# A two-layer long-convolution and MLP kernel: k read as plain rows, four tokens to a partition, ten products on GpSimd, a new written order

## The chip, the core and the metric

The kernel runs on one core of a Trainium2 chip. Its engines are TensorE (PE in the profile, with its weight loads as PEld), VectorE (DVE), ScalarE (ACT), GpSimd (POOL) and SyncE (SP), which here only issues DMAs. The metric is device time in microseconds (us); lower is better.

## The reference

Two blocks are applied twice to x, which starts as q (2048 tokens of 512 channels, bf16).

```python
k_shift = sum over t in 0..3 of k_pad[:, t:t+S] * shift_k[:, 3-t]     # k_pad: 3 zeros, then k
kv = k_shift * v
y  = irfft(rfft(kv, 2S) * rfft(ssm_k, 2S))[:S] + kv * ssm_D          # long causal convolution
A(x) = layernorm(x) * y
B(x) = gelu(layernorm(x) @ w1 + b1) @ w2 + b2                        # 512 -> 1376 -> 512
x = x + A(layernorm(x)); x = x + B(layernorm(x));  the same two lines again
```

y doesn't depend on x: both layers use the same y.

## The kernel before

The 2048 tokens are cut into four blocks j of 512 tokens. Filter block j and kv block j are each brought to 512 frequencies. Output block j is the sum over a of the product of kv block a and filter block j - a, brought back to time. The names below are the pieces of the list `ORDER`, in which the order on every engine is written out by hand: a piece is `name.engine`, and engines S, A, D, G, P are SP, ACT, DVE, POOL and PE. Each engine takes its instructions strictly in that order. PE writes to four PSUM buffers P0 to P3.

- `lK`, `lk`, `lv`, `lx` load blocks of the filter, k, v and q. `lT` loads the tables of the direct transform, `lF`, `lW`, `lM`, `lY` the others. `lk` is a transposing DMA from DRAM (line 330): channels come to lie on partitions.
- `KT` turns the filter block on PE (line 383), `KTe` copies it out. `dt` adds ssm_D to the filter's first token, so the kv * ssm_D term costs nothing further.
- `kv` (line 405) forms the shifted sum on PE: k against diagonal matrices `DG` of the four taps, 56 matmuls a half block, in 64x64 tiles. `kvm` (line 416) multiplies by v; the result is u.
- For blocks 0 and 1, `KD` and `UD` (line 442) transform the filter and u directly, with eight 128x512 matmuls a piece.
- For blocks 2 and 3 the transform has two steps. `KS`, `US` (line 467) do the first; `Kw`, `Uw` write its result to DRAM, `Kr`, `Ur` read it back in another order, and `KW`, `UW` (line 483) do the second step. This write and read is called a round trip below.
- `ks` (line 427) swaps real and imaginary halves of a filter block by DMA from SBUF to SBUF.
- `T` (line 503) are the products of one u block with one filter block, all on DVE. `V` (line 516) sums them and does the first inverse step; `Vw`, `Vr` are its round trip; `Y` (line 535) the second step.
- In layer l, block g has number i = 2g + l. `sa`/`sb` (line 260 and on) are the layer norm statistics on DVE, `pa`/`pb` (line 272) the inverse root on POOL, `aa`/`ab` (lines 280, 282) the normalising on ACT or DVE, `ga` (lines 593, 594) x + norm * y. `dw` writes the normalised block to DRAM and `dr` (line 605) reads it back transposed; block 0 of layer 0 is turned on PE instead (`LT`, line 576).
- `m1` (line 617) and `ge` (line 624) are the first MLP matrix and gelu, `m2` (line 637) the second. `re` (line 645) adds the residual on DVE; for i = 0 and 1 PE adds it with an identity matmul (line 634) and `re` is a plain copy (line 241 on ACT). `st` stores.

Partition p of k, u, the filter and x holds tokens 8(p mod 64) + 4(p div 64) + 0..3 of its block: a load or store needs two DMAs of 64 partitions.

Of the kernel before, what the change touches and what calls it, by code (L numbers as in the profile page):

```python
# [16 lines left out]
ls.A id.G lK0.S lk0.S lD.A lT2.A ke0.G id2.D lb.G lT0.A lY.A lT3.A w3.S lx0.S lT1.A dg.D lv0.S sg.G lx2.S KT00.P0 lK1.S  # L17
KT01.P1 KT00e.D KT01e.A dt.D lF.A kv01.P2 ke1.G KD02.P3 KD03.P0 KD02e.D sa00.D kv00.P1 KD03e.A lM.A ks011.S KD00.P3
sa02.D ks010.S lx1.S KD01.P0 KD00e.A kvm00.D kvm01.D KT10.P3 KD01e.A sa40.D UD02.P1 ks000.S lk1.S sa42.D pa40.G UD03.P2
UD02e.A pa00.G KT10e.A lK3.S ks001.S T002.D UD01.P0 pa42.G lv1.S sa22.D UD03e.A w2.S KD11.P1 UD01e.A ke2.G pa02.G T003.D  # L20
aa40.A KD10.P3 pa22.G T001.D UD00.P2 aa42.A aa22.D KD10e.D kv11.P0 UD00e.A KD11e.D V01.P3 V02.P2 kvm11.D ks101.S kv10.P1
V02e.A ks100.S T000.D V01e.A V03.P0 lK2.S KD13.P2 lv2.S kvm10.D V03e.A aa02.A Vw01.S V00.P3 T100.D KD12.P0 V00e.A
UD10.P1 KD12e.D aa00.A Vw00.S KD13e.D UD11.P3 UD10e.A sa20.D ks110.S UD13.P0 UD11e.A ks111.S lW.A T110.D UD12.P2 UD13e.A
Vr00.S Vr01.S lk2.S KT20.P1 T101.D UD12e.A KT20e.A w1.S w4.S Y00.P3 T111.D V10.P0 Y00e.A Y01.P2 V11.P1 Y01e.A ga00.D
KS23.P3 V11e.A V13.P2 ga02.D V10e.A V12.P1 KS23e.A sb00.D kv20.P0 Vw10.S V13e.A KS21.P3 sb02.D V12e.A KT30.P2 KS21e.A
Vw11.S kv21.P1 kvm20.D pb02.G KT30e.A KS20.P3 pb00.G ab02.D cb.G pa20.G ab00.D LT02.P0 KS20e.A KS22.P2 kvm21.D on0.G
LT02e.A Vr10.S LT00.P3 Vr11.S LT00e.D US21.P1 KS22e.A US20.P0 US20e.D m102.P3 US21e.A Kw21.S T213.D US22.P2 ge02.A
US23.P0 m103.P1 aa20.D US23e.A US22e.D Y11.P3 ge03.A m101.P0 T210.D Uw21.S Kw20.S Uw20.S Y11e.A T211.D Y10.P2 ge01.A
m105.P1 Y10e.D m100.P3 ge05.A ga20.D m104.P0 ge00.A Kr2.S T212.D KS31.P2 ge04.A KS30.P1 sb20.D KS32.P3 m200.P0 KS32e.A
Ur2.S KS31e.A sb22.D pb20.G KS30e.A ab20.D pb22.G dw20.S ke3.G ab22.D KW20.P3 dw22.S re00.A KW22.P2 KW20e.D Kw30.S  # L30
KW23.P1 KW23e.A KS33.P0 KW22e.D UW23.P3 UW23e.A KW21.P1 sa10.D UW21.P2 KS33e.A m202.P3 dr2.S UW21e.A KW21e.D pa10.G
aa10.A T221.D ks200.S ks201.S T223.D lv3.S Kw31.S m125.P0 re02.A UW20.P2 UW22.P1 sa12.D m120.P3 UW22e.A UW20e.A m124.P1
T201.D pa12.G ge25.A aa12.A T200.D V21.P2 T222.D m123.P0 V21e.A Kr3.S ga10.D lk3.S m122.P2 ge23.A T220.D ge24.A m121.P0
T203.D ge22.A V20.P1 T202.D ge20.A V23.P2 sb10.D V20e.A V22.P3 ge21.A Vw20.S lx3.S sb12.D pb10.G kv30.P1 V22e.A on2.G
V23e.A pb12.G KW33.P0 kvm30.D kv31.P3 KW33e.A Vw21.S KW32.P2 kvm31.D KW30.P1 ab12.A m220.P0 ab10.D KW30e.A sa62.D dw12.S
dw10.S KW32e.A Vr20.S T323.D pa62.G US33.P3 re20.D US32.P1 m222.P2 US32e.A dr1.S T313.D US33e.A T320.D Uw31.S Vr21.S
T311.D US30.P0 re22.D US31.P1 US30e.A m112.P3 aa62.D US31e.A T322.D KW31.P2 ge12.A Y20.P0 Uw30.S m110.P1 sa32.D KW31e.A
m115.P3 Y20e.A ks301.S T312.D Y21.P2 ge10.A m111.P0 Ur3.S sa30.D Y21e.A ks300.S m113.P1 ge15.A T310.D pa30.G ge11.A
on1.G m114.P2 ga40.D pa32.G ge13.A ge14.A UW30.P3 sb42.D on4.G UW33.P0 UW31.P1 UW30e.A m212.P2 UW33e.A T301.D pb42.G
UW31e.A sb40.D ab42.A T321.D pb40.G dw42.S m210.P3 re12.A T300.D ab40.A T330.D T303.D aa30.A dw40.S T331.D UW32.P0  # L40
T302.D V31.P1 UW32e.A dr4.S aa32.D V30.P2 T332.D V31e.A re10.A T333.D V32.P0 V30e.A sa60.D Vw30.S V33.P1 V32e.D pa60.G
m141.P3 V33e.A ga30.D Vw31.S m142.P2 ge41.A aa60.D m140.P0 sb30.D ge42.A m143.P1 Vr31.S ge40.A sb32.D pb30.G Vr30.S
m144.P3 ge43.A pb32.G ab32.D m145.P2 ge44.A ab30.D dw32.S Y31.P0 ge45.A dw30.S Y30.P1 st10.S Y31e.A Y30e.D m242.P3
st12.S ga60.D dr3.S sb62.D m240.P2 sb60.D pb60.G pb62.G ab60.D m131.P0 ab62.D re40.D dw62.S dw60.S m130.P1 sa50.D
m134.P2 ge30.A re42.D pa50.G ge31.A dr6.S m133.P1 sa52.D ge34.A m135.P3 aa50.D ge33.A pa52.G m132.P0 aa52.A m165.P2
m163.P1 ge32.A ga50.D ge65.A m162.P0 ge35.A ge63.A sb50.D m164.P2 sb52.D m160.P3 pb52.G m161.P1 ge60.A on3.G ab52.D
# [13 lines left out]
T202:622 T212:1286 T222:558 vs21:1415 T203:1463 T213:966 T223:1030 ziV2:1254 y2:878 x2:750 T300:1254 T310:1574 T320:1478  # L60
T330:1190 vs30:312 T301:518 T311:1414 T321:1286 T331:1222 T302:910 T312:1510 T322:1446 T332:582 vs31:518 T303:280
T313:1382 T323:1350 T333:550 ziV3:0 y3:88 x3:1030 W1:344 W2:128 ln0:1190 lt0:1222 h0:558 ln2:646 lt2:646 h2:878 ln4:1062
lt4:248 h4:430 ln6:1318 lt6:32 h6:430 ln1:1383 lt1:1542 h1:910 ln3:216 lt3:0 h3:216 ln5:304 lt5:518 h5:0 ln7:304 lt7:88
h7:430
# [17 lines left out]
def _make_tables():  # L82
# [11 lines left out]
    for h in range(2):  # L94
        rows = slice(64 * h, 64 * h + 64)
        F[rows, 0, 0], F[rows, 0, 1] = c, s
        F[rows, 1, 0], F[rows, 1, 1] = s, -c

# [77 lines left out]
def kernel(ctx: ExitStack, tc: tile.TileContext, A_q, A_k, A_v, A_shift_k, A_ssm_k, A_ssm_D,  # L176
# [75 lines left out]
    class Norm:  # L252
# [10 lines left out]


# [6 lines left out]
        def root(self, a, b):  # L271
            nc.gpsimd.tensor_tensor(self.rs[:, a:b], self.rs[:, a:b], mhalf[:, a:b], ALU.pow)  # L272

        def apply(self, eng, dst, xg, a, b):
            if eng == "A":
                nc.vector.scalar_tensor_tensor(out=self.nm[:, a:b], in0=self.mv[:, a:b, 0], scalar=-1.0, in1=self.rs[:, a:b],  # L276
                                               op0=ALU.mult, op1=ALU.mult)
# [26 lines left out]
    with tc.tile_pool(name="ps", bufs=1, space=bass.MemoryType.PSUM) as ps:  # L304
# [21 lines left out]
        PAD = 16  # L326
        KW = PAD + L

        def k_turn(it, j):
            nc.sync.dma_start_transpose(at(f"kT{j}", PAD, [[KW, CT], [1, L]]), k_d[L * j:L * j + L, :])  # L330
        q_d, k_d, v_d, out_d = (t.flatten_outer_dims() for t in (A_q, A_k, A_v, out))
        lk, edge = [], []
        for j in range(NB):
            lk.append(add(f"lk{j}", "S", [], lambda it, j=j: k_turn(it, j), kb=[512], xbar=True, bufs=[buf(f"kT{j}", CT * KW)]))

            def left(it, j=j):
                dst = at(f"kT{j}", PAD - 4, [[KW, CT], [1, 4]])
                if j == 0:
                    nc.gpsimd.memset(dst, 0.0)
# [344 lines left out]
```

## Time and profile before

| | us |
|---|---|
| median of 3 runs | 276.62 (274.1 to 276.82) |
| the profiled execution, its own time | 278.13 |
| its span, first to last instruction | 276.4 |
| outside the span | 1.7 |
| PE busy in the span | 245.8 |
| DVE busy | 174.8 |
| ACT busy | 143.0 |
| POOL busy | 34.9 |
| mean granted PE clock | 0.983 |

The profile shows one execution. Busy PE time isn't PE at full rate: matmuls overlap, so counts of instructions in a stretch say more than busy time does. A line number is that of the kernel before; several pieces can share a line where a helper records them (line 241 is every copy on ACT, line 313 every plain load).

### The profile page before, as it was taken

How to read it: one execution, taken by the hardware profiler on the slowest of the kernel's cores; microseconds unless marked ns; L12 is line 12 of the kernel's file. 1: busy time of each engine (PE TensorE's matmuls, PEld its weight loads, DVE VectorE, ACT ScalarE, POOL GpSimd, SP SyncE). 2: the span in 40 equal slices, each digit the busy share in tenths (PEclk: the TensorE clock that was granted, in tenths of full speed). 3: DMA queues.
4: the chain of work that ended last, by engine and by line, in shares of the span. 5: the costliest groups of instructions: out<-in, count | busy, mean ns of one | idle time of the engine just before them, and what ended most of it. 6: DMA issues, size and time to landing. Idle time of an engine off the chain costs nothing.

```text
span 276.4 us, 4777 instructions
## 1 busy us (share of the span) xinstructions
PE 245.8 (89%) x1921; PEld 119.7 (43%) x1944; DVE 174.8 (63%) x306; ACT 143.0 (52%) x184; POOL 34.9 (13%) x59
## 2 busy tenths in 40 slices
PE   1179998979999959999999799999999999999991
PEld 1045546444834424446433245444444444444440
DVE  0209659779887875895979598948955148611041
ACT  1102458576888666695578575570394502802700
POOL 4000330000400200010205120112104011200000
PEclk9999999997999999999999799999999999999998
DMA  7999797999677979797989323593410230051034
GB/s 124 147 238 233 187 239 205 275 302 222 220 225 239 235 218 225 175 221 217 191 266 219 84 75 80 170 287 76 123 34 1 76 78 0 31 121 38 2 86 104
DMA packets 46794, 43.46 MB, mean 157 GB/s; under 512 B 25554, under 2 KB 41524, under 8 KB 46004
## 3 DMA queue, kind: packets, MB, share of 16 engines
q1 hardware_dynamic: 45010, 41.63, 59.3%
q10 hardware_dynamic: 1682, 1.53, 3.4%
q8 instruction: 15, 0.25, 0.4%
q0 software_dynamic: 80, 0.00, 0.1%
q14 instruction: 7, 0.06, 0.1%
HBM read 19.03 MB, written 14.16 MB: 120 GB/s over the span
## 4 chain that ended last, share of the span: by engine, by line
PE 59%; DMA 25%; SPq 5%; DVE 4%; ACT 3%; issue 2%; DVEq 0%; ACTq 0%
PE p L637 22%; PE p L617 21%; DMA arena<-in_A_k_dram 8%; PE p L516 4%; PE p L405 4%; DMA lnd<-arena 3%; PE p L442 3%; DMA arena<-zdU 3%; DMA zdV<-arena 2%; DMA arena<-zdV 2%; DMA arena<-lnd 2%; DMA arena<-in_A_v_dram 2%; SPq L427 2%; DMA arena<-arena 2%; ACT arena L241 1%
## 5 line engine op out<-in xcount | busy, mean ns | idle before, releaser
L241 ACT ACTIVATE arena<-p 128x1024 bf16<-128x1024 f32 (+2 forms) x68 | 69.0, 1062 | 47.9 <-DMA Ft<-tabF 14.2
L624 ACT ACTIVATE arena<-p,B 128x512 bf16<-128x512 f32 (+1 forms) x88 | 54.3, 690 | 52.9 <-PE p L617 51.4
L637 PE MATMUL p<-arena 128*128 128x512 bf16 (+1 forms) x345 | 79.4, 384 | 0.5
L617 PE MATMUL p<-arena 128*128 128x512 bf16 (+1 forms) x342 | 77.7, 379 | 1.5 <-DMA arena<-lnd 0.5
L503 DVE TENSOR_TENSOR arena<-arena 128x2048 bf16<-128x2048 bf16 (+1 forms) x36 | 47.2, 1338 | 17.4 <-DMA arena<-arena 10.6
L637 PEld LDWEIGHTS <-arena 128*128 128x128 bf16 (+1 forms) x352 | 34.5, 99 | 43.7 <-issue 4.0
L617 PEld LDWEIGHTS <-arena 128*128 128x128 bf16 (+1 forms) x352 | 34.6, 100 | 43.4 <-issue 3.8
L272 POOL TENSOR_TENSOR lrs<-lrs,mhalf 128x2 f32<-128x2 f32 x32 | 27.2, 855 | 188.2 <-DVE lrs L266 96.9
L260 DVE BATCH_NORM_STATS2 lst<-arena 128x6 f32<-128x512 bf16 x64 | 41.0, 681 | 2.5 <-ACT arena L241 2.3
L645 DVE TENSOR_TENSOR arena<-p,arena 128x1024 bf16<-128x1024 f32 (+1 forms) x14 | 14.9, 1071 | 36.6 <-PE p L637 36.5
L442 PE MATMUL p<-arena 128*128 128x512 bf16 x123 | 30.0, 397 | 0.4 <-issue 0.2
L280 ACT ACTIVATE arena<-arena,lnm,lrs 128x512 bf16<-128x512 bf16 x26 | 19.7, 814 | 11.7 <-DVE lnm L276 11.6
L405 PE MATMUL p<-arena 64*64 64x128 bf16 (+3 forms) x448 | 15.1, 286 | 8.4 <-DMA arena<-in_A_k_dram 8.4
L243 DVE CAST arena<-p 128x1024 bf16<-128x1024 f32 x9 | 10.9, 1222 | 18.4 <-PE p L442 12.1
L516 PE MATMUL p<-arena,Mt 64*64 64x512 bf16 x320 | 20.3, 392 | 1.1 <-DVE arena L448 0.7
L442 PEld LDWEIGHTS <-arena 128*128 128x128 bf16 x128 | 12.6, 102 | 16.4 <-issue 3.5
L405 PEld LDWEIGHTS <-arena 64*64 64x64 bf16 x448 | 14.7, 210 | 10.4 <-DMA arena<-in_A_k_dram 9.1
L282 DVE TENSOR_SCALAR arena<-arena,lmv,lrs 128x512 bf16<-128x512 bf16 x38 | 14.6, 430 | 4.3 <-POOL lrs L272 4.2
L516 PEld LDWEIGHTS <-Mt 64*64 64x64 bf16 x320 | 9.3, 110 | 10.7 <-issue 3.8
L383 PE MATMUL p<-IDt,arena 128*64 128x128 bf16 x128 | 8.6, 297 | 5.6 <-DMA arena<-in_A_ssm_k_dram 5.6
L416 DVE TENSOR_TENSOR arena<-p,arena 128x1024 bf16<-128x1024 f32 x8 | 9.7, 1220 | 4.2 <-PE p L405 2.9
L593 DVE TENSOR_TENSOR arena<-arena 128x2048 bf16<-128x2048 bf16 (+1 forms) x9 | 9.9, 1102 | 3.3 <-ACT arena L280 2.7
(38 smaller groups left out, 84.0 us busy)
## 6 DMA issues: line engine op xcount, KB each, us to landing
zdV<-arena SPq DMA_DIRECT2D x8, 512.0 KB, 3.8
arena<-zdV SPq DMA_DIRECT2D x8, 512.0 KB, 4.8
lnd<-arena SPq DMA_DIRECT2D x14, 256.0 KB, 2.3
arena<-in_A_ssm_k_dram SPq DMA_DIRECT2D x4, 512.0 KB, 4.7
arena<-in_A_q_dram SPq DMA_DIRECT2D x8, 256.0 KB, 4.7
arena<-in_A_v_dram SPq DMA_DIRECT2D x8, 256.0 KB, 5.7
arena<-arena SPq DMA_DIRECT2D x16, 128.0 KB, 4.0
zdK<-arena SPq DMA_DIRECT2D x4, 512.0 KB, 5.1
```

The costliest lines, as they stand in the source:

```text
L241: nc.scalar.activation(dst, src, AF.Copy)
L260: nc.vector.bn_stats(lst[:, i, :], xg[:, i, :])
L272: nc.gpsimd.tensor_tensor(self.rs[:, a:b], self.rs[:, a:b], mhalf[:, a:b], ALU.pow)
L280: nc.scalar.activation(dst[:, i, :], xg[:, i, :], AF.Identity, bias=self.nm[:, i:i + 1], scale=self.rs[:, i:i + 1])
L405: nc.tensor.matmul(o[64 * R:64 * R + 64, r, m0:m9, c2, :], at(f"kT{j}", cc * KW + PAD + 4 * R + d, [[8, 64]], 64 * r, 64), at("DG", (cc * ...
L442: nc.tensor.matmul(o[:, r, :], at(f"TD{i}", (n * 2 + r) * P, [[1, P]]), at(src, n * D, [[1, D]]), start=n == 0, stop=n == 3)
L503: nc.vector.tensor_tensor(at(t, 0, [[2 * D * w, 2], [1, 2 * D * w]]), at(f"U{a}", 2 * i * D, [[0, 2], [1, 2 * D * w]]), at(f"K{kk}", 2 * i ...
L516: nc.tensor.matmul(o[64 * r:64 * r + 64, e, :], Mt[64 * e:64 * e + 64, 2 * i + r, s, :], at(f"T{j}{a}{i // TW[j]}", (s * 2 * TW[j] + 2 * ( ...
L617: nc.tensor.matmul(o[0:m, x, :], at("W1", ct * F + ft * P, [[1, m]]), at(LT, ct * 4 * P, [[1, 4 * P]]), start=ct == 0, stop=ct == CT - 1)
L624: nc.scalar.activation(at(HT, ft * 4 * P, [[1, 4 * P]], 0, m), o[0:m, x, :], AF.Gelu_apprx_tanh, bias=B1[0:m, ft:ft + 1])
L637: nc.tensor.matmul(o[:, x, :], at(HT, ft * 4 * P + t * P, [[1, P]], 0, m), at("W2", ft * D, [[1, D]], 0, m), start=ft == 0 and i not in RE ...
L645: nc.vector.tensor_tensor(xs, psum(pe, [2, D])[:, 0:len(tt), :], xs, ALU.add)
```

## The change

1. k is loaded as plain rows, four tokens (4 KB) a partition, by one DMA a block. PE turns it: new pieces `kt`, 64 transposes of 128x128 in all, and their copies `kte`. The edge copy `ke` now waits for `kte` of the block before.
2. Partition p of k, u and the filter holds tokens 4p to 4p+3. `KT` needs 64 transposes of 128x128 in place of 128 of 128x64. x keeps its order, loaded and stored by one DMA with a three-step pattern.
3. `kv` uses 64x128 tiles: 28 matmuls a half block in place of 56.
4. `KS` and `US` use the full 128x128 array: 4 and 2 matmuls a piece in place of 8 and 4 in 64x64 tiles.
5. Ten products `T` are on POOL.
6. The residual for i = 0 and 1 is added on DVE (`re`), and the identity matmuls go.
7. The product of mean and inverse root that ACT's normalising needs is made by two small operations, one on DVE in every `sa`/`sb` and one on POOL in every `pa`/`pb`; before it was one DVE operation where ACT normalised.
8. `gd`, a one-element gelu on ACT, comes ahead of the first `ge`.
9. `ORDER` and `PLACE` (where each buffer lies in SBUF) are new. On DVE there are 17 copies of 128x1024 f32 results in place of 9, five bf16 copies of 128x1024 in place of two, and two of 128x2048 in place of none; DVE normalises 16 halves in place of 19.

SP's queue at the program's start, before: arena is the one SBUF buffer, in_A_ssm_k the filter, in_A_k is k, in_A_q is x, line 427 the swaps.

```order
L313 DMA arena<-in_A_ssm_k_dram 128x4x512
L330 DMA_TRANSPOSE arena<-in_A_k_dram 128x4x512
L313 DMA arena<-in_B_w_dram 96x512
L313 DMA arena<-in_A_q_dram 64x2048 x2
L313 DMA arena<-in_A_v_dram 64x2048 x2
L313 DMA arena<-in_A_q_dram 64x2048 x2
L313 DMA arena<-in_A_ssm_k_dram 128x4x512
```

And of the change, the same place (tabT is a table of the direct transform; the other three of the four, and v, stand on ACT's queue):

```order
L316 DMA arena<-in_A_ssm_k_dram 128x4x512
L316 DMA arena<-in_A_ssm_D_dram 1x512
L316 DMA arena<-tabT 128x1024
L316 DMA arena<-in_A_q_dram 128x1x2048
L316 DMA arena<-in_A_k_dram 128x2048
L316 DMA arena<-in_A_q_dram 128x1x2048 x2
L316 DMA Mt<-tabM 128x1024
```

The transposing load of k is gone from second place; plain k stands fifth, behind a table and a block of x.

SP's queue where filter block 2 comes back from its round trip, before (zdK2, zdU2 and zdK3 are the DRAM buffers of round trips, lnd2 the normalised block i = 2, line 605 its transposing read, line 427 the swaps of filter block 2):

```order
L313 DMA arena_63<-zdK2_134 64x1x4096 x2
L313 DMA arena_63<-zdU2_138 64x1x4096 x2
L313 DMA lnd2_126<-arena_63 128x2x512 x2
L313 DMA zdK3_135<-arena_63 128x4x512
L605 DMA_TRANSPOSE arena_63<-lnd2_126 128x4x512
L427 DMA arena_63<-arena_63 32x4096 x4
```

And of the change:

```order
L316 DMA arena_63<-zdK2_134 64x1x4096 x2
L316 DMA arena_63<-zdU2_138 64x1x4096 x2
L316 DMA arena_63<-in_B_b2_dram 1x512
L316 DMA arena_63<-in_B_w2_dram 96x512
L316 DMA zdK3_135<-arena_63 128x4x512
L436 DMA arena_63<-arena_63 32x4096 x4
L316 DMA lnd2_126<-arena_63 128x2x512
```

The four swaps stand ahead of the block's writes and its transposing read; before they stood behind them.

POOL's queue in the last third of the convolution, of the change (line 274 is the inverse root, line 275 the new product, line 512 a product `T`, line 619 a memset; lrs6 belongs to `pa` of i = 3, lrs12 to `pa` of i = 6):

```order
L274 TENSOR_TENSOR lrs6_95<-lrs6_95,mhalf_73 128x2
L275 TENSOR_TENSOR lnm6_96<-lnm6_96,lrs6_95 128x2
L512 TENSOR_TENSOR arena_63<-arena_63 128x2048
L274 TENSOR_TENSOR lrs6_95<-lrs6_95,mhalf_73 128x2
L275 TENSOR_TENSOR lnm6_96<-lnm6_96,lrs6_95 128x2
L512 TENSOR_TENSOR arena_63<-arena_63 128x2048
L619 MEMSET arena_63 1x512
L512 TENSOR_TENSOR arena_63<-arena_63 128x2048
L274 TENSOR_TENSOR lrs12_113<-lrs12_113,mhalf_73 128x2
```

Before, only inverse roots and memsets stood here; now three products (`T302`, `T330`, `T332`) do. In `ORDER` the pieces of PE from there on are `UW32 m140 V31 V33 V30 V32`, where `V30` reads `T330` and `V32` reads `T302` and `T332`.

The diff's core:

```diff
-RES_PE = {0, 1}
+TG = {(1, 0), (1, 1), (2, 0), (2, 1), (2, 2), (3, 0), (3, 1), (3, 2), (3, 3)}
+RES_PE = set()
...
-        t = 8 * (p % 64) + 4 * (p // 64) + n
+        t = 4 * p + n
...
         def stats(self, xg, a, b, twice):
...
+            nc.vector.tensor_scalar_mul(self.nm[:, a:b], self.mv[:, a:b, 0], -1.0)
...
         def root(self, a, b):
             nc.gpsimd.tensor_tensor(self.rs[:, a:b], self.rs[:, a:b], mhalf[:, a:b], ALU.pow)
+            nc.gpsimd.tensor_tensor(self.nm[:, a:b], self.nm[:, a:b], self.rs[:, a:b], ALU.mult)
         def apply(self, eng, dst, xg, a, b):
-            if eng == "A":
-                nc.vector.scalar_tensor_tensor(out=self.nm[:, a:b], in0=self.mv[:, a:b, 0], scalar=-1.0, in1=self.rs[:, a:b],
-                                               op0=ALU.mult, op1=ALU.mult)
...
-    def rows(t, j, h, n0=0, n9=4):
-        return apf(t, t.offset + (L * j + 4 * h + n0) * D, [[8 * D, 64], [1, (n9 - n0) * D]])
+    def lines(t, j):
+        return apf(t, t.offset + L * j * D, [[4 * D, P], [1, 4 * D]])
+    def rows(t, j, n0=0, n9=4):
+        return apf(t, t.offset + (L * j + n0) * D, [[4 * D, 2], [8 * D, 64], [1, (n9 - n0) * D]])
...
-            nc.sync.dma_start_transpose(at(f"kT{j}", PAD, [[KW, CT], [1, L]]), k_d[L * j:L * j + L, :])
+        lk = [load(f"lk{j}", lambda j=j: [(at(f"kr{j}", 0, [[1, 4 * D]]), lines(k_d, j))], engines="SA" if j == 0 else "S", kb=[512],
+                   bufs=[buf(f"kr{j}", 4 * D)]) for j in range(NB)]
...
-                            for R in range(2):
-                                nc.tensor.transpose(o[64 * R:64 * R + 64, n, cc, :], at(f"Kraw{j}", cc * L + 4 * R + c * nn + n, [[8, 64]]), IDt[:])
+                            nc.tensor.transpose(o[:, n, cc, :], at(f"Kraw{j}", cc * L + c * nn + n, [[4, P]]), IDt[:])
...
+                            nc.tensor.transpose(o[:, cc, n, :], at(f"kr{j}", (c * nn + n) * D + cc * P, [[1, P]]), IDt[:])
...
-                                for R in range(2):
-                                    nc.tensor.matmul(o[64 * R:64 * R + 64, r, m0:m9, c2, :], at(f"kT{j}", cc * KW + PAD + 4 * R + d, [[8, 64]], 64 * r, 64),
-                                                     at("DG", (cc * KS + m0 - d) * 64, [[64, m9 - m0], [1, 64]], 64 * r, 64),
+                                nc.tensor.matmul(o[:, r, m0:m9, c2, :], at(f"kT{j}", (4 * cc + d % 4) * KI + 4 + d // 4, [[1, P]], 64 * r, 64),
+                                                 at("DG", (cc * KS + m0 - d) * 64, [[64, m9 - m0], [1, 64]], 64 * r, 64),
...
                             for R in range(2):
-                                for p in range(2):
-                                    nc.tensor.matmul(o[64 * p:64 * p + 64, R, :], Ft[64 * R:64 * R + 64, f, p, :], at(t, n * D, [[1, D]], 64 * R, 64),
+                                nc.tensor.matmul(o[:, R, :], Ft[:, f, R, :], at(t, n * D, [[1, D]]), start=s == 0, stop=s == len(terms) - 1,
...
+                            e = nc.vector if it["eng"] == "D" else nc.gpsimd
+                            e.tensor_tensor(at(t, 0, [[2 * D * w, 2], [1, 2 * D * w]]), at(f"U{a}", 2 * i * D, [[0, 2], [1, 2 * D * w]]),
+                                            at(f"K{kk}", 2 * i * D, [[8 * D, 2], [1, 2 * D * w]]), ALU.mult)
...
+        gd = add("gd", "A", [cb], lambda it: nc.scalar.activation(gz[:], B1[:, 0:1], AF.Gelu_apprx_tanh), us=1.5)
```

More of the change, by code (lines that the diff above doesn't have):

```diff
@@ L16 @@
 ORDER = """
[L17 to L46, printed above, removed]
@@ L60 @@
[L60 to L64, printed above, removed]
+Kraw0:0 Kraw1:440 Kraw2:96 Kraw3:344 kr0:256 kr1:622 kr2:408 kr3:1094 u0:376 u1:1255 u2:1126 u3:1430 TD0:472 TD1:1094
@@ L93, in _make_tables @@
     c, s = np.cos(ang) * same, np.sin(ang) * same
[L94 to L97, printed above, removed]
+    for R in range(2):
+        on = (R4 == R)[:, None]
+        F[:, 0, R, 0], F[:, 0, R, 1] = c * on, s * on
+        F[:, 1, R, 0], F[:, 1, R, 1] = s * on, -c * on
     W = np.zeros((128, 8, 64))
```

166 lines of the change are left out of this document (103 added, 63 removed).

## The prediction

> **What bounds the kernel now.** I read the busy shares first, then stretches of the span, then the chain that ended last.
>
> ```profile
> span 276.4 us, 4777 instructions
> PE 245.8 (89%) x1921; PEld 119.7 (43%) x1944; DVE 174.8 (63%) x306; ACT 143.0 (52%) x184; POOL 34.9 (13%) x59
> ```
>
> PE is the engine to count. The stretches show what a full matmul costs and where PE isn't full (columns: stretch, sum, then PE, PEld, DVE, ACT, POOL busy, clock, DMA):
>
> ```profile
> 0.00:10.00 10.00, 2.18 (x32) 2.00 (x32) 2.59 (x5) 2.31 (x2) 2.95 (x15) 1.00 0.92 138
> 10.00:20.00 10.00, 4.49 (x62) 2.99 (x64) 0.00 (x0) 0.00 (x0) 0.20 (x1) 1.00 1.06 197
> ...
> 90.00:100.00 10.00, 8.67 (x70) 3.60 (x70) 7.90 (x18) 6.06 (x7) 1.62 (x3) 1.00 0.99 244
> 100.00:110.00 10.00, 8.43 (x51) 3.74 (x52) 6.26 (x12) 6.11 (x7) 0.69 (x1) 1.00 0.89 214
> ...
> 150.00:160.00 10.00, 7.98 (x37) 2.98 (x36) 6.74 (x15) 6.18 (x9) 3.89 (x4) 0.83 0.47 103
> ...
> 200.00:210.00 10.00, 9.95 (x47) 4.74 (x47) 6.64 (x16) 7.50 (x13) 0.93 (x2) 1.00 0.15 31
> ```
>
> At 200 us PE is full: 47 matmuls of 128x512 in 9.95, **0.212 us** each. Such a stretch shortens only by fewer matmuls or an earlier start. Before it PE is idle for 13.3 us of the first 20, for 2.9 between 90 and 110, and for 2.0, with a clock of 0.83 besides, from 150. The chain (start, length, what) names causes:
>
> ```profile
> 1.34 13.91 DMA arena<-in_A_k_dram
> 15.29 2.15 PE p L405 x47
> ...
> 50.70 6.81 DMA zdV<-arena
> 57.59 0.35 SPq L313
> 57.98 6.51 DMA arena<-zdV
> ...
> 95.73 6.35 DMA lnd<-arena
> 102.14 2.03 SPq L605
> ...
> 106.48 5.24 DMA arena<-arena
> ...
> 146.36 7.48 DMA arena<-zdU
> ```
>
> They are the transposing load of k; V's first round trip; a transposing read with the filter's swaps queued behind it; U's last round trip. The change touches all four.
>
> **Part 1, the start.**
>
> ```profile
> 5.57 2.18 PE L383 MATMUL p<-IDt,arena 128*64 128x128 bf16 x32 [5.57 <-DMA arena<-in_A_ssm_k_dram]
> ...
> 8.54 0.41 DVE L388 TENSOR_TENSOR arena<-arena 1x512 bf16<-1x512 bf16 x1
> ...
> 18.20 4.78 PE L442 MATMUL p<-arena 128*128 128x512 bf16 x14 [0.22 <-issue]
> ```
>
> The filter is ready for `KD` at 8.54 + 0.41 = 8.95, but in the order before, `kv01` stands ahead and waits for k until 15.29. Now `KD03` and `KD00` stand first, and k comes after. The first 14 matmuls take 4.78, 0.341 each, so 16 from 8.95 end at 14.4. Lost by then is what isn't work at full rate: 14.4 - 16 x 0.212 - 1.2 (the transposes of `KT`) = 9.8. Before, PE reaches the end of the same row at 22.98 with 32 transposes (2.1), `kv01` (1.9) and 16 matmuls (3.4) done: 15.6 lost. That is 5.8 gained if nothing else is late. Two things can be: ahead of k's last byte now stand about 1.8 MB (filter, two or three tables, a block of x), and at the rows' 138 and 197 GB/s 2.3 MB land between 11.7 and 16.7; and the tables:
>
> ```profile
> arena<-tabT ACTq DMA_DIRECT2D x4, 256.0 KB, 12.2
> ```
>
> If `lT3` takes those 12.2 us, `KD03` starts at about 13 and 1.7 is left of the gain. I take **-4**, bounds -5.8 and 0; a loss I exclude, since plain k stands behind no more bytes than the transposed one and PE has work ahead of it.
>
> **Part 2, PE's work.**
>
> ```profile
> 57.90 2.13 PE L383 MATMUL p<-IDt,arena 128*64 128x128 bf16 x32
> ...
> 73.05 1.86 PE L405 MATMUL p<-arena 64*64 64x256 bf16 x56
> ...
> 75.28 0.62 PE L576 MATMUL p<-IDt,arena 128*128 128x128 bf16 x8
> ...
> 90.24 1.49 PE L467 MATMUL p<-arena,Ft 64*64 64x512 bf16 x24
> ```
>
> Transposes: 128 at 2.13/32 = 0.067 become 128 (half filter, half k) at 0.62/8 = 0.078, +1.4. Shifted sum: 448 at 1.86/56 = 0.033 become 224 whose price no row shows. No lower than 0.033, the price of a smaller tile, and no higher than 0.078, a full tile with as many columns; two 64-row tiles can stand in the array at once, so I take 0.04: 9.0 in place of 14.9, -5.9 (bounds -7.5 and +2.6). First step of the two-step transform: 96 at 1.49/24 = 0.062 become 48 full ones at 0.212, +4.2. Eight identity matmuls go, -1.7. Sum **-2.0**, bounds -3.6 and +6.5.
>
> **Part 3, waits for DMAs.**
>
> ```profile
> 61.87 0.62 PE L535 MATMUL p<-arena,Yt 128*64 128x512 bf16 x4 [1.84 <-DMA arena<-zdV]
> ```
>
> V's first trip took 50.70 to 64.49. Between its last V piece and `Y00` PE had five dense pieces (8 x 0.212 each) and `KT20`, 10.6 us; now it has two `kv`, two `KS`, four `UD`, `kt20` and `KT30`, 2.2 + 1.7 + 6.8 + 2.4 = 13.1. That is 2.5 more cover against a wait of 1.84: **-1.8**, bounds -2 and 0. Filter block 2's swaps now stand ahead of the block's writes (6.35) and transposing read (2.03); of the 2.9 idle between 90 and 110, and of what followed it until the swap landed at 111.7, I take **-1.7**, bounds -5 and +1 (the swaps delay the writes, and with them `m120`). U's last trip: from `US` to `UW30` PE had five `m1` pieces of 1.7, a half one, two `Y` and a `KW`, 10.6; now it has `m220` (22 x 0.212 = 4.7), five `m1` and a half one, 14.0. That covers the 2.0 idle at 150 and the lost clock (0.17 of 8): **-3**, bounds -3.5 and 0. Together **-6.5**, bounds -10.5 and +1.
>
> **Part 4, DVE and POOL.**
>
> ```profile
> L503 DVE TENSOR_TENSOR arena<-arena 128x2048 bf16<-128x2048 bf16 x32 | 38.2, 1219 | 13.4 <-DMA arena<-arena 7.2 <-ACT arena L241 4.7 <-DMA zdU<-arena 1.1
> L503 DVE TENSOR_TENSOR arena<-arena 128x4096 bf16<-128x4096 bf16 x4 | 9.1, 2290 | 4.0 <-DMA arena<-arena 3.4 <-ACT arena L241 0.6
> L282 DVE TENSOR_SCALAR arena<-arena,lmv,lrs 128x512 bf16<-128x512 bf16 x38 | 14.6, 430 | 4.3 <-POOL lrs L272 4.2
> L645 DVE TENSOR_TENSOR arena<-p,arena 128x1024 bf16<-128x1024 f32 x10 | 12.2, 1223 | 22.0 <-PE p L637 22.0
> L243 DVE CAST arena<-p 128x1024 bf16<-128x1024 f32 x9 | 10.9, 1222 | 18.4 <-PE p L442 12.1 <-ACT arena L624 2.7 <-issue 1.8
> L243 DVE COPY arena<-p 128x1024 bf16<-128x1024 bf16 x2 | 1.4, 686 | 0.9 <-PE p L576 0.9
> L276 DVE SCALAR_TENSOR_TENSOR lnm<-lmv,lrs 128x2 f32<-128x2 f32 x13 | 2.0, 153 | 0.9 <-POOL lrs L272 0.9
> ```
>
> DVE loses nine products of 1.22 and one of 2.29, 13.3, and three halves of normalising, 3 x 2 x 0.384 = 2.3. It gains 8 casts (9.8), three bf16 copies and two of double size (4.8), four residual additions (4.9) and 32 - 13 small operations (2.9): **6.8 us more**, not less. It works 6.3 to 7.9 of each ten around 100, so most fits; of what doesn't, +1.5, bounds 0 and 5. ACT, with eight copies and four residuals less, binds nothing.
>
> ```profile
> L624 ACT ACT_TABLE_LOAD x1 | 1.3, 1283 | 0.7 <-issue 0.7
> ...
> out_dram<-arena SPq DMA_DIRECT2D x8, 64.0 KB, 2.1
> ```
>
> Two edits I cost at nothing. `gd` moves the table load ahead of the first gelu, beside `m102` and `Y11` on PE; without that cover it is the 1.28 it was. The last store is one DMA in place of two of 64 KB; its 2.1 stays at the end either way.
>
> What a product costs on POOL no row shows. Nearest are its memsets, and how POOL and DVE meet:
>
> ```profile
> L607 POOL MEMSET arena<- 1x512 bf16 x8 | 4.2, 538 | 0.4
> L339 POOL MEMSET arena<- 128x16 bf16 x1 | 0.1, 108 | 0.0
> ...
> 132.00 1.22 DVE L503 TENSOR_TENSOR arena<-arena 128x2048 bf16<-128x2048 bf16 x1
> ...
> 132.17 1.60 POOL L272 TENSOR_TENSOR lrs<-lrs,mhalf 128x2 f32<-128x2 f32 x1 [6.94 <-DVE lrs L269]
> 172.33 0.69 POOL L272 TENSOR_TENSOR lrs<-lrs,mhalf 128x2 f32<-128x2 f32 x1 [11.62 <-DVE lrs L269]
> ```
>
> From 16 to 512 elements a memset gains 0.43, 0.87 ns an element, so one stream of 2048 takes 1.9 us; two reads and a write one after another would take 5.4. I take 3, nearer the single stream. `V22` has 2.6 us of PE work after the place of `T202`; `V32` has 7.0 after that of `T330`, and waits for two products and a memset (0.54). At 3 that is 6.5: covered, and `V22` waits 0.4. The inverse root takes 0.69 alone and 1.60 when a product of DVE is running: one of the two stands still. Eleven units of 3 us on POOL are 33 us; DVE's remaining products alone, 32 us in some 190, meet them for about 5.5 us, of which I put half on DVE's side and, with the roots queued behind products, +2.1 on the path. With `V22`'s 0.4, **+4** in all for part 4, bounds 0 and +18 (the upper one is worked out below).
>
> The Trainium skill, SBUF — State Buffer, section "Who interferes with whom", says that a DVE operation with two SBUF inputs and a GpSimd operation that reads SBUF exclude each other for a whole instruction; the 1.60 against 0.69 agrees. By that rule whichever starts second also pays the whole rest of the other, so a DVE product could stand up to a POOL product's length.
>
> **Sum.** -4 - 2.0 - 6.5 + 4 = -8.5. Against the profiled execution's own 278.13 that is 269.6; it lies 1.5 above the median of the runs, 276.62, so from there **268**.
>
> **Rivals.** *Slower, by POOL:* a product takes 5.4. Then `V32` waits 2 x 5.4 + 0.54 - 7.0 = 4.3 and `V22` 2.8; 59 us on POOL meet DVE's products for 10 and hold DVE and the roots some 7 longer than in the forecast, 4 of it, by the same share, on the path; and three products written before the roots `pb20` cost 3 x 5.4 = 16.2 against 13 us of PE work, 3 late. 4.3 + 2.8 + 4 + 3 = 14 on top: 282. From about 4.5 us a product it eats the gain. For it: no row has two inputs this long on POOL. Against: the single stream's 1.9.
>
> *No gain:* the tables come as late as they do now (-1.7 in place of -4) and a `kv` matmul costs 0.067, so that a half block takes what it took (+6): -8.5 + 2.3 + 6 = -0.2, 276. For it: all four table loads show the 12.2, and a 64-row tile that loads 128 columns may not pair up. Against: one table now has ACT's queue to itself at the start.
>
> The Trainium skill, GPSIMD Engine Reference, section "Elementwise — side-by-side cycle accounting", gives 4497 ns for an addition of two f32 tensors of 2048 elements on GpSimd. As an estimate for these bf16 products it would put the kernel at the turning point, near 276.
>
> *Faster still:* every wait of part 3 goes and the start gains its 5.8: -5.8 - 3.6 - 10.5 + 2 = -18, 258.
>
> **Chances.** Forecast (263 to 273) 0.52, faster still 0.14, no gain 0.12, slower 0.22; within 1% of 276.6 (273.9 to 279.4) is about what a measurement of this kernel can't tell from no change. So faster 0.66, same 0.12, slower 0.22. The range runs from 259 to 281: it leaves out half of each outer case.
>
> **What would show it.** PE's first 128x512 matmul near 9 us, not 17; V's and U's trips without idle PE; a POOL product near 3 us; DVE's products at 1.22 still. It is wrong if products on POOL last over 4.5 us, if DVE is busy 9 of each ten from 20 to 150 with PE idle behind it, or if `kv` takes more than the 1.86 us it took.

## The result, and the profile after

The changed kernel takes **317.2 us** (median of 4 runs, 315.98 to 318.53) against 276.72 for the kernel before on the same chip: 1.15 times as long, 95% interval 1.140 to 1.160. The forecast was 268, range 259 to 281. The profiled execution took 317.8, its span is 316.1. The ratios in this document leave out executions over 1.5% above the fastest of their kernel, so a ratio can differ by a few us from the quotient of two medians.

The busy shares of the changed kernel:

```profile
span 316.1 us, 4309 instructions
PE 250.4 (79%) x1664; PEld 117.2 (37%) x1664; DVE 194.7 (62%) x326; ACT 136.9 (43%) x179; POOL 89.7 (28%) x101
```

The span grew by 39.7, PE's busy time by 4.6. So PE waits; the question is where. Stretches of the same trace (columns: stretch, sum, PE, PEld, DVE, ACT, POOL busy, clock, DMA share, GB/s):

```profile
10.00:20.00 10.00, 3.37 (x12) 1.15 (x10) 0.00 (x0) 1.02 (x1) 0.00 (x0) 0.92 0.15 58
20.00:30.00 10.00, 8.37 (x88) 5.13 (x88) 4.58 (x14) 3.78 (x5) 2.08 (x8) 0.74 0.26 87
30.00:40.00 10.00, 4.15 (x13) 1.62 (x14) 4.00 (x8) 0.70 (x1) 1.08 (x3) 0.66 0.49 133
...
170.00:180.00 10.00, 4.22 (x19) 1.57 (x18) 9.97 (x11) 2.93 (x4) 6.36 (x4) 0.77 0.25 71
200.00:210.00 10.00, 10.00 (x51) 4.34 (x50) 7.37 (x16) 2.09 (x4) 1.12 (x3) 1.00 0.39 105
...
289.53:316.10 26.57, 0.00 (x0) 0.00 (x0) 0.00 (x0) 0.00 (x0) 0.00 (x0) 0.53 0.13 47
```

There are three holes: 10 to 40, 170 to 180, and 26.57 us at the end, behind the last residual addition, in which no engine computes. The same stretch of the kernel before:

```profile
271.10:276.40 5.30, 0.00 (x0) 0.00 (x0) 0.00 (x0) 0.00 (x0) 0.00 (x0) 0.77 0.35 84
```

Now read the column of DMA shares. From 10 to 20 it is 0.15 where before it was 1.06, and in the end stretch 0.13. A share of 0.13 of 16 engines is 2.1 engines. In these holes DMAs are what is waited for, and yet most DMA engines stand idle (no row of a hole has a share above 0.49). In the holes the granted clock falls too, to 0.74 and 0.66 between 20 and 40, and what PE does there takes longer: the 16 transposes of k, the row at 21.27 below, take 1.89, where they take 1.06 in the best kernel further on.

SP's own timeline says which DMAs (start, length, queue, line, what; the length is how long SP was held in issuing):

```profile
6.99 10.51 SPq L316 DMA_DIRECT2D arena<-in_A_q_dram  x2
17.55 9.75 SPq L316 DMA_DIRECT2D Mt<-tabM  x1
...
161.89 0.54 SPq L316 DMA_DIRECT2D arena<-in_A_q_dram  x1
167.07 9.09 SPq L617 DMA_TRANSPOSE arena<-lnd  x1
...
203.16 2.09 SPq L617 DMA_TRANSPOSE arena<-lnd  x1
...
270.56 36.43 SPq L316 DMA_DIRECT2D out_dram<-arena  x10
```

Each hole has loads of x (in_A_q) or stores of the output in it. The chain of what ended last gives the two waits behind the loads:

```profile
28.79 18.12 DMA arena<-in_A_ssm_k_dram
...
167.07 11.06 DMA arena<-lnd
```

The next filter block lands at 46.91, and PE turns it only then. At 167 the transposing read, issued behind the fourth block of x, takes 11.06, and SP is held for 9.09 where the next such read, at 203, holds it for 2.09. The output is 2048 x 512 x 2 bytes = 2.1 MB; at the 47 GB/s of the end stretch that is 44.6 us, and from the first store's issue at 270.56 to the end are 45.5. The stores alone set the end.

Rows that answer those of part 1 and part 4 of the prediction, from PE's timeline and from the groups:

```profile
8.11 5.26 PE L451 MATMUL p<-arena 128*128 128x512 bf16 x16 [0.66 <-DVE arena L378]
21.27 1.89 PE L394 MATMUL p<-IDt,arena 128*128 128x128 bf16 x16 [7.90 <-DMA arena<-in_A_k_dram]
...
46.96 3.60 PE L373 MATMUL p<-IDt,arena 128*128 128x128 bf16 x32 [4.33 <-DMA arena<-in_A_ssm_k_dram]
```

```profile
L512 POOL TENSOR_TENSOR arena<-arena 128x2048 bf16<-128x2048 bf16 x9 | 42.4, 4713 | 22.2 <-PE p L475 10.7 <-DVE arena L246 4.7 <-ACT arena L244 3.9
L512 DVE TENSOR_TENSOR arena<-arena 128x2048 bf16<-128x2048 bf16 x23 | 37.2, 1661 | 0.2 <-ACT arena L244 0.2
```

The first full matmuls start at 8.11, near the forecast (8.95); k comes 7.9 late behind a block of x. A product on POOL takes 4.71 in the mean, not 3 (the shortest single one 4.06), and DVE's own products take 1.66 in place of 1.22.

### The profile page after: what moved, and what is told of

Its sections match the earlier page's. It is cut to its first block, busy times and chain, and to the rows that moved or that the text cites. A ratio compares the mean times of both kernels' runs of the same rounds, so it can differ in the third digit from the quotient of the medians.

```text
span 316.1 us, 4309 instructions
## 1 busy us (share of the span) xinstructions
PE 250.4 (79%) x1664; PEld 117.2 (37%) x1664; DVE 194.7 (62%) x326; ACT 136.9 (43%) x179; POOL 89.7 (28%) x101
## 4 chain that ended last, share of the span: by engine, by line
PE 52%; DVE 16%; DMA 13%; SPq 7%; issue 3%; ACTq 0%; POOL 0%; ACT 0%; DVEq 0%
PE p L629 20%; PE p L649 20%; SPq L316 7%; DMA arena<-in_A_ssm_k_dram 6%; DMA arena<-lnd 5%; DVE arena L512 5%; PE p L525 3%; PE p L451 3%; DVE lst L263 2%; DVE arena L246 2%; DVE arena L605 2%; DMA arena<-tabT 2%; DVE arena L425 1%; DVE arena L606 1%; PE p L475 1%
## 5 line engine op out<-in xcount | busy, mean ns | idle before, releaser
L244 ACT ACTIVATE arena<-p 128x1024 bf16<-128x1024 f32 (+2 forms) x56 | 58.5, 1084 | 57.2 <-PE p L451 20.7
L274 POOL TENSOR_TENSOR lrs<-lrs,mhalf 128x2 f32<-128x2 f32 x32 | 23.4, 732 | 128.5 <-DVE lrs L271 75.9
L512 POOL TENSOR_TENSOR arena<-arena 128x2048 bf16<-128x2048 bf16 (+1 forms) x10 | 50.3, 5036 | 25.8 <-PE p L475 10.7
L657 DVE TENSOR_TENSOR arena<-p,arena 128x1024 bf16<-128x1024 f32 (+1 forms) x18 | 19.5, 1102 | 38.3 <-PE p L649 29.4
L451 PE MATMUL p<-arena 128*128 128x512 bf16 x128 | 34.5, 427 | 6.9 <-DVE arena L425 6.2
L280 ACT ACTIVATE arena<-arena,lnm,lrs 128x512 bf16<-128x512 bf16 x32 | 24.2, 807 | 35.6 <-POOL lnm L275 35.5
L246 DVE CAST arena<-p 128x1024 bf16<-128x1024 f32 x17 | 20.4, 1220 | 8.6 <-PE p L544 6.2
L282 DVE TENSOR_SCALAR arena<-arena,lmv,lrs 128x512 bf16<-128x512 bf16 x32 | 12.2, 427 | 5.3 <-POOL lrs L274 5.3
L373 PE MATMUL p<-IDt,arena 128*128 128x128 bf16 x64 | 6.6, 290 | 9.9 <-DMA arena<-in_A_ssm_k_dram 9.9
L475 PE MATMUL p<-arena,Ft 128*128 128x512 bf16 x48 | 12.2, 380 | 2.0 <-DVE arena L425 2.0
L394 PE MATMUL p<-IDt,arena 128*128 128x128 bf16 x64 | 5.1, 242 | 7.9 <-DMA arena<-in_A_k_dram 7.9
```

Of the source, the lines that this page charges most:

```text
L244: nc.scalar.activation(dst, src, AF.Copy)
L246: nc.vector.tensor_copy(dst, src)
L280: nc.scalar.activation(dst[:, i, :], xg[:, i, :], AF.Identity, bias=self.nm[:, i:i + 1], scale=self.rs[:, i:i + 1])
L451: nc.tensor.matmul(o[:, r, :], at(f"TD{i}", (n * 2 + r) * P, [[1, P]]), at(src, n * D, [[1, D]]), start=n == 0, stop=n == 3)
L512: e.tensor_tensor(at(t, 0, [[2 * D * w, 2], [1, 2 * D * w]]), at(f"U{a}", 2 * i * D, [[0, 2], [1, 2 * D * w]]), at(f"K{kk}", 2 * i * D, [[ ...
```

## The experiments

**Theory A:** a DMA whose DRAM pattern leads with a step of two runs on two DMA engines, holds up what stands behind it on SP's queue, and costs all of the loss. **Theory B:** POOL's long products, and VectorE and the roots held up by them, cost most of it.

### Two DMAs of 64 partitions again

Loads and stores of x get the two DMAs of the kernel before; all else is the change. Then the loads alone, and the stores alone.

```diff
-  (at(f"x{j}", 0, [[1, 4 * D]]), rows(q_d, j))                     # [[4D, 2], [8D, 64], [1, 4D]]
+  (at(f"x{j}", 0, [[1, 4 * D]], 64 * h, 64), half(q_d, j, h))      # [[8D, 64], [1, 4D]], h = 0, 1
```

> The change with one edit undone: every load of x and every store is again two DMAs of 64 partitions each. Theory A (the one-DMA form with its outer step of two moves at some 50 GB/s, and blocks SP's queue behind it): the tail after the last addition falls from 26.6 us to about 5, and the start's loss from 30 to about 11, so 317 - 21 - 19 = 277. Theory B (the ten products on POOL, 4.1 to 5.9 us each with DVE's products held up to 5 us, are what the time went to, and the loads are hidden behind them): only the tail goes, 296 or more.

> Only the loads of x as two DMAs; the stores stay single. A: 317 - 19 = 298, first KT10 transposes near 28 us, not 47. B: 312 or more, since the later waits take the place of the early one.

> Only the stores as two DMAs; the loads stay single. A and B: 317 - 21 = 296, the end about 5 us after the last addition. If this and the loads alone add up to both together, the two losses are independent.

Measured: both 272.12 (ratio to before 0.990, interval 0.986 to 0.994), loads alone 294.07, stores alone 299.34 (one run each). Against 317.2 the loads are worth 23.1, the stores 17.9, both 45.1. Theory A holds, and B can't have been most of the loss. The two single edits add up to 41.0 of the 45.1, so the loss at the start and that at the end are nearly independent, as far as one run of each tells. Of the 43.4 us by which the span shrinks, 19.0 lie before the second filter block is turned (27.96 for 46.96) and 22.2 behind the last addition (it ends at 268.37 of 272.7, so 4.3 for 26.57).

### The products too

As before, and all ten products of POOL on VectorE.

```diff
-T100.G  T213.G  T212.G  T211.G  T222.G  T202.G  T303.G  T302.G  T330.G  T332.G
+T100.D  T213.D  T212.D  T211.D  T222.D  T202.D  T303.D  T302.D  T330.D  T332.D
```

> Loads and stores as two DMAs each, and all ten products on DVE, the order otherwise the change's. A: DVE gains 13 us of products and loses some 11 us of being held (26 products at 1.22 in place of 1.66), so 1 to 6 us below the run with halves alone. B: 15 us or more below it.

Measured: **262.14**, ratio 0.956 (0.947 to 0.965): 10.0 below the kernel with the products on POOL. Three of its four executions took 261.73 to 262.52, the fourth, which is the profiled one, 1413.04; there 44 full matmuls of PE take 58.02, 1.32 each in place of 0.212, and no run shows why. The time is between the two forecasts, nearer to neither; the products on POOL have a price of their own. A second set, for a profile at the usual speed and beside the next kernels:

> The kernel with two DMAs of 64 partitions for x and all ten products on VectorE, run once more for its profile, and beside the kernel before: 262 (260 to 264), ratio 0.94 to 0.965. In the profile VectorE's products should last 1.22 each again in place of 1.66, its busy share of each ten between 40 and 170 should stand below 9, and PE's waits for products and copies on VectorE after 140 should be below 1 us each.

Measured 262.19, ratio 0.951 (0.945 to 0.958). VectorE's products are at 1.217 again, and PE waits less, as expected; but VectorE's busy share isn't below 9 of ten, as I had written. Page, stretch and group of this kernel:

```profile
PE 240.4 (92%) x1638; PEld 114.1 (44%) x1664; DVE 190.4 (73%) x336; ACT 136.6 (52%) x179; POOL 39.5 (15%) x91
...
150.00:160.00 10.00, 9.95 (x127) 5.48 (x121) 9.93 (x14) 2.65 (x5) 0.00 (x0) 1.00 0.22 74
...
L515 DVE TENSOR_TENSOR arena<-arena 128x2048 bf16<-128x2048 bf16 x32 | 37.7, 1217 | 0.2 <-ACT arena L244 0.2
```

The same of the kernel with two DMAs for x and the products on POOL, and what PE waits for there:

```profile
PE 246.7 (90%) x1664; PEld 116.0 (43%) x1664; DVE 193.6 (71%) x326; ACT 136.8 (50%) x179; POOL 89.4 (33%) x101
...
150.00:160.00 10.00, 5.08 (x48) 1.95 (x47) 9.96 (x11) 4.15 (x6) 5.57 (x3) 0.90 0.00 0
...
L515 DVE TENSOR_TENSOR arena<-arena 128x2048 bf16<-128x2048 bf16 x23 | 36.9, 1652 | 0.2 <-ACT arena L244 0.2
...
140.00 7.35 DVE L515 TENSOR_TENSOR arena<-arena 128x2048 bf16<-128x2048 bf16 x3
140.02 5.11 POOL L515 TENSOR_TENSOR arena<-arena 128x2048 bf16<-128x2048 bf16 x1
...
157.49 0.69 PE L528 MATMUL p<-arena,Mt 64*64 64x512 bf16 x8 [3.10 <-DVE arena L515]
```

Nine products of 1.217 and one of 2.28, 13.2 us, were taken from VectorE, and it is busy 3.2 us *longer*: 16.4 us of its busy time is standing still, 10.0 of that in its own 23 products (1.652 for 1.217). At 140 one sees it: a product of POOL (5.11) begins with a run of three on VectorE, and these last 7.35 in place of 3 x 1.2. PE then waits for VectorE's products, and no wait of PE in this trace is put down to POOL; PE does half of its work from 150 to 160. The two executions traced differ by 12.0 us of span. PE is idle for 5.7 of them: its waits for VectorE are 8.9 in place of 5.2, and 2.3 come at the start, where k was late. For the other 6.3 it is busy longer with the same work, at a mean granted clock of 0.971 in place of 0.993: the clock is 0.87, 0.85, 0.90 and 0.76 in the stretches from 70, 90, 150 and 160, where the kernel with its products on VectorE has 1.00 (its one low stretch is 0.83, from 80).

### Work on GpSimd that nobody waits for

> The kernel of e8_dve_again (all products on VectorE, two DMAs for x) with eleven units of extra work on GpSimd: at each place where the change has a product on GpSimd, GpSimd multiplies a scratch tile of its own onto itself, as many elements as the product has, and nobody waits for the result. VectorE still does all products itself. Theory L (the 10 us that the products on GpSimd cost are PE waiting for late products): 262 to 264. Theory X (they are VectorE and the inverse roots held up by GpSimd's long instructions, whoever needs their results): 268 to 274, with VectorE's products above 1.5 us in the mean and single ones near 5.

```diff
+xs = const.tile([P, 1024], BF16, name="xs")
-T100.G
+T100.D X100.G      # X: nc.gpsimd.tensor_tensor(xs[:], xs[:], xs[:], ALU.mult), twice (four times for T100); the same at the other nine
```

Measured: **283.56**, ratio 1.029 (1.021 to 1.037); 21.4 above the kernel without the scratch work. Theory X has the direction, and the size is beyond its range. Page and groups:

```profile
PE 244.7 (87%) x1638; PEld 115.7 (41%) x1664; DVE 213.4 (76%) x336; ACT 136.8 (49%) x179; POOL 90.3 (32%) x114
...
L523 POOL TENSOR_TENSOR xs<-xs 128x1024 bf16<-128x1024 bf16 x22 | 49.3, 2243 | 1.2
L520 DVE TENSOR_TENSOR arena<-arena 128x2048 bf16<-128x2048 bf16 x32 | 48.7, 1556 | 0.2
L282 DVE TENSOR_SCALAR arena<-arena,lmv,lrs 128x512 bf16<-128x512 bf16 x32 | 22.5, 746 | 5.3 <-POOL lrs L274 5.3
```

VectorE is busy 23.0 us longer for the same work (213.4 for 190.4): products at 1.56, normalising at 0.75 in place of 0.43. The time rises by nearly as much, and the trace says where: PE's waits for VectorE are 21.1 in all, in place of 5.2. The late inverse roots, which queue behind the scratch work, may have their part in the 21.4. The waits that the trace puts down to them hardly grow (VectorE's stay at 5.3, ScalarE's go from 22.7 to 24.3), but no run parts them from the rest. So no product on POOL has to be late for POOL's work to cost time. 21.4 less the 13.2 of products that the change takes off VectorE is 8.2, near the 10.0 that moving them costs; this counts VectorE's time in full, which no run tests.

### The leading step, by itself

All products are on VectorE in these three, so that POOL plays no part, and x comes by single DMAs. Only the counts of the DRAM pattern differ: 2 x 64 as in the change, 4 x 32, 16 x 8. With 4 and 16 the tokens of x lie on other partitions than those of y, so x meets the y of another token: these two kernels time the pattern and don't compute the reference.

```diff
-[[4 * D, 2], [8 * D, 64], [1, 4 * D]]
+[[4 * D, 16], [64 * D, 8], [1, 4 * D]]     # or [[4 * D, 4], [16 * D, 32], [1, 4 * D]]
```

> The change with all ten products on VectorE and x loaded and stored by single DMAs as the change has it, but the three-step DRAM pattern leads with 16 steps in place of 2 (16, then 8, then 4 KB rows). This permutes the tokens within each block of x, in the loads and the stores alike; all work stays. Theory A (the leading count decides over how many DMA engines a transfer spreads): as with two DMAs of 64 partitions and all products on VectorE, 262, range 260 to 266, and a load of 512 KB in 3 to 5 us. Theory B (a single DMA with three steps is slow whatever its counts, or one DMA is slower than two): 300 to 307, with the 10 us a load.

> The kernel of e6_one_dma_outer16 with a leading count of 4 (4, then 32, then 4 KB rows); tokens are permuted within a block likewise. Theory A (a transfer spreads over as many engines as the leading count): a load of 512 KB moves at twice the pace of the change's, about 5.5 us in place of 11, and at a quarter of that of a leading 16 where nothing else is in flight; the tail after the last residual addition falls from 26.6 us to about 10 (two queued blocks at half the time, less what hides them), and the loads stall little. Time between 268 and 282. Theory B (only two against many matters): 260 to 264.

> The change with all ten products on VectorE and nothing else undone: single DMAs with a leading step of two stay. Theory X (what the products on GpSimd cost adds to what the DMAs cost): 317 - 10 = 307. Theory Y (with the DMAs slow there is slack that hides the products on GpSimd): 313 to 317.

Measured, for 2, 4 and 16: **316.01, 282.47, 260.43** (ratios 1.141, 1.023 and 0.946, intervals 1.127 to 1.156, 1.013 to 1.033, 0.938 to 0.954). The stretch from 10 to 20 us and that behind the last addition, first of the kernel with 2:

```profile
10.00:20.00 10.00, 4.72 (x13) 1.44 (x11) 0.00 (x0) 1.02 (x1) 0.00 (x0) 0.88 0.14 55
...
287.95:314.50 26.55, 0.00 (x0) 0.00 (x0) 0.00 (x0) 0.00 (x0) 0.00 (x0) 0.55 0.13 47
```

With 4:

```profile
10.00:20.00 10.00, 3.77 (x17) 1.65 (x16) 1.49 (x4) 1.02 (x1) 0.00 (x0) 0.91 0.61 166
...
271.48:282.90 11.42, 0.00 (x0) 0.00 (x0) 0.00 (x0) 0.00 (x0) 0.00 (x0) 0.62 0.22 83
```

With 16:

```profile
10.00:20.00 10.00, 9.89 (x100) 5.65 (x101) 8.97 (x23) 4.48 (x5) 3.16 (x11) 1.00 1.01 294
...
254.95:258.40 3.45, 0.00 (x0) 0.00 (x0) 0.00 (x0) 0.00 (x0) 0.00 (x0) 0.88 0.16 45
```

Behind the last addition the traffic goes by the leading count: 47 GB/s at a share of 0.13 (2.1 of 16 engines), 83 at 0.22 (3.5 of 16). Neither "one DMA" nor "three steps" is slow: with 16 it is as fast as two DMAs of 64 partitions, or a little faster (260.43 against 262.19 in the same set, intervals overlapping). With 4 the time lies just above what I had written (268 to 282), and the end stretch is 11.4 where about 10 was expected.

The Trainium skill, DMA: Bandwidth & Descriptors, section "Why a DMA increments its semaphore by 16 and not by 1", states the rule: the largest number of engines up to 16 is used that divides the slowest dimension, other than 1, of both access patterns. The shares above agree for 2 and 4.

The last of the three has a second lesson. With the products on VectorE it takes 316.01, and the change itself 317.2 (ratios 1.141 and 1.150, intervals overlapping): in the kernel as changed, the products on POOL cost nothing that is measured. Theory Y is right, X wrong. From 167 to 178 PE waits for the transposing read in the change (from 165 to 176 with the products on VectorE), and I read it so that in this time the change's VectorE catches up: from 170 to 180 it is busy for 9.97 of ten, where the other kernel's is for 6.22. No run tests that alone. The 10 us show only once the DMAs are mended.

### The single DMA in the kernel before

> The kernel before, with one edit alone: x is loaded, and the result stored, by single DMAs whose DRAM pattern has three steps and a leading step of two, as in the change. Theory A (such a DMA is slow wherever it stands, since it spreads over few engines): the loads and stores cost here what they cost in the change's order, 18 for the stores and 15 to 23 for the loads, so 276 + 33 to 41 = 309 to 317, with the last 25 us or so nearly empty on every engine. Theory B (the new order puts x ahead of k, and only that makes the loads dear): the stores' 18 alone, 294. Theory C (the cost is of the new order altogether): 276.

```diff
-(at(f"x{j}", 0, [[1, 4 * D]], 64 * h, 64), rows(q_d, j, h)) for h in range(2)
+(at(f"x{j}", 0, [[1, 4 * D]]), rows1(q_d, j))                      # [[4D, 2], [8D, 64], [1, 4D]]; stores likewise
```

Measured: **330.8** (324.93 to 335.57), ratio 1.186 (1.170 to 1.202): by the ratio some 51 us (47 to 56) for this one edit, no less than in the new order. B and C fall; A has the cause right and the size too small. The chain and the last stretch of this kernel:

```profile
14.42 25.96 DMA arena<-in_A_ssm_k_dram
41.66 10.96 SPq L333
...
302.94:327.20 24.26, 0.00 (x0) 0.00 (x0) 0.00 (x0) 0.00 (x0) 0.00 (x0) 0.59 0.13 47
```

The same two holes: a filter block takes 25.96 behind blocks of x, SP is held for 10.96 at a transposing load of k (line 333 here), and the end stretch is 24.26.

### Five copies from VectorE to ScalarE

> The kernel of e8_dve_again with five copies of PE's results (KS22e, UD10e, UW30e, UW32e, V31e) moved from VectorE to ScalarE. If VectorE, 19.9 of each 20 us busy from 40 to 60 and from 120 to 160, is what is left in the way of PE there, PE's waits for VectorE (1.9 at 46.86 and 1.3 at 66.66 in e8_dve_again) shrink and the time is 259 to 261. If VectorE is only just full, off the path, it stays at 262; if ScalarE's queue makes the copies late, up to 265.

> The kernel of e8_dve_again once more, beside the one with the copies moved: 262 (261.5 to 263).

```diff
-KS22e.D  UD10e.D  UW30e.D  UW32e.D  V31e.D
+KS22e.A  UD10e.A  UW30e.A  UW32e.A  V31e.A
```

Measured: 261.72 against 263.21 for the same kernel without it, ratios to before 0.949 (0.941 to 0.956) and 0.955 (0.949 to 0.961), so not told apart: the second kernel alone took 262.19 in one set and 263.21 in another. From 40 to 60 VectorE is busy 17.17 in place of 19.43, but PE's two waits named in the forecast are still 1.9 and 1.3: they are for the shifted sum's multiplication (`kvm`), not for these copies, and in VectorE's order the copies `KS22e` and `UD10e` stand behind the `kvm` of the first wait. What is taken from a full VectorE shortens PE's wait only if it stands ahead of what PE waits for.

## Why the prediction was wrong, and where it was right

- **The step that failed** stands among the "two edits I cost at nothing": "The last store is one DMA in place of two of 64 KB; its 2.1 stays at the end either way." The loads of x, which the change alters in the same way, got no term at all: part 1 counted the block of x ahead of k by its bytes, at the rows' 138 and 197 GB/s, and excluded a loss. I took the duration of a DMA by its bytes, from a row of a DMA with another pattern; no row of the trace before had a leading step of two, so the price was unknown and needed bounds from both sides, as the other unknown costs had. Measured: 45.1 us with the rest of the change, 53.8 with the products on VectorE (316.01 for 262.19), some 51 in the kernel before. The range, without this term, ended at 281. Of the prediction's own signs of being wrong one came, a product on POOL of over 4.5 us; it isn't what made the kernel slower.
- **Part 1, the start (-4):** right once x comes by two DMAs. Ahead of the second filter block's transposes, there are 32 transposes of full tiles, 56 full matmuls and 56 of the shifted sum: 32 x 0.078 + 56 x 0.212 + 56 x 0.035 = 16.3. They begin at 25.66 in the best kernel, and at 27.96 in the traced execution of the kernel with the products on POOL: 9.4 and 11.6 lost, against 15.6 in the prediction. So 6.2 and 4.0 gained, around the forecast and its best bound of 5.8. The difference isn't POOL's: in the second execution PE waits 3.06 for k, and with the products on POOL and only the loads mended it waits 0.43 and the transposes begin at 25.94. In the change they begin at 46.96: 30.7 lost.
- **Part 2, PE's work (-2.0):** the unknown price, 0.04 for a 64x128 matmul of the shifted sum, is 0.035:

```profile
13.27 1.06 PE L397 MATMUL p<-IDt,arena 128*128 128x128 bf16 x16
...
16.54 1.95 PE L417 MATMUL p<-arena 64*128 64x256 bf16 x56 [0.48 <-DVE arena L246]
...
25.66 1.95 PE L376 MATMUL p<-IDt,arena 128*128 128x128 bf16 x32
...
L478 PE MATMUL p<-arena,Ft 128*128 128x512 bf16 x45 | 12.1, 380 | 1.4 <-DVE arena L428 1.3
```

  That makes 224 x 0.035 = 7.8, not 9.0, and the sum -3.2, within its bounds. The transposes came out cheaper too: 0.066 each in the row of k and 0.061 in that of the filter, where I took 0.078 from a run of eight. That is 8.1 for the 128 in place of 10.0, and the sum is near -5, beyond its bound of -3.6. The last row (all are of the kernel with all products on VectorE) shows that the first step of the transform now has full tiles; its mean of 380 overlaps with neighbours and says nothing of the rate.
- **Part 3, waits for DMAs (-6.5):** the mechanism was right. PE's waits for the trips of U and V (total, times, longest) in the kernel before:

```profile
PE p L483 <- DMA arena<-zdU: 3.7, 2, 2.0
PE p L535 <- DMA arena<-zdV: 2.0, 2, 1.8
```

  And with two DMAs for x and the products on VectorE, where no row for V is left:

```profile
PE p L494 <- DMA arena<-zdU: 0.7, 1, 0.7
```

  Both waits for V are those of its first trip. Of the two for U, 1.97 at 153.87 is the last trip's; the other, 1.71 at 100.83, is block 2's, inside the idle time from 90 to 110 that I had given to the swaps, and the 0.7 that is left is block 2's too. So the 4.0 of the two trips that I forecast are gone. The stretch from 150 to 160, 7.98 at a clock of 0.83 before, is 9.95 at 1.00 there, 1.4 more by the prediction's 0.17 of 8: 5.4, where I had 4.8. Of the 1.7 for the swaps these rows show 1.0; how the rest divides no run shows.
- **Part 4, DVE and POOL (+4, of which 1.5 for DVE's added work):** mis-sized. A product takes 4.7, nearer the upper end (5.4) than the single stream (1.9) that I chose. "From about 4.5 us a product it eats the gain" was the better sentence: 272.12 lies some 2.7 below the kernel before (ratio 0.990), and 10.0 above the same kernel with its products on VectorE. What I wrote of its mechanism was half right. I had VectorE and POOL hold each other up, but put late products beside it, 0.4 for `V22` and, in the rival, 4.3 for `V32`; no wait of PE in that kernel is put down to POOL, and PE waits for VectorE. VectorE stands still for 16.4 us, where I gave 2.8 to its side, and the clock that PE loses by waiting had no term. The Trainium skill's 4497 ns, GPSIMD Engine Reference, section "Elementwise — side-by-side cycle accounting", is near the measured 4684 to 4713, and its rule of exclusion, SBUF — State Buffer, section "Who interferes with whom", agrees with the 7.35 for three products.
- **The sum:** without the failed term, -8.5 stood against a measured -2.7 with the products on POOL (ratio 0.990); without POOL's part, -11 against -13.4 (ratio 0.951). The change held a gain of some 13 us, of which one idea took back 10 and another, unpriced, 45 to 54.

## What to carry to other kernels

A DMA is priced by how many engines it uses before its bytes: read the leading counts of both patterns (the runs here vary that of the DRAM side alone), and where no row of the trace has such a pattern, give it bounds as for any unknown operation, with what is queued behind it. A stretch in which a DMA is waited for at a DMA share of 0.13, 2 engines of 16, points to this fault. Moving work from a full VectorE to GpSimd freed nothing here, where both ran at once: count the time that each holds the other up, and not the time moved.
